# One attention and two-layer feed-forward kernel: state loads on other queues, ScalarE's opening held in order, two weight pieces converted earlier

## The chip, the cores and the metric

The kernel runs on one core of one Trainium2 chip. The metric is device time in microseconds (us) of one execution; three runs of the kernel before gave 1241.46, 1243.35 and 1245.03 us, so the median is 1243.35 us. The core has a matrix engine (TensorE, PE in the profile, with its weight loads as PEld), a vector engine (VectorE, DVE), a scalar engine (ScalarE, ACT), GpSimd (POOL) and SyncE (SP). SP, ACT and POOL can issue transfers (DMAs) between memory and the on-chip buffers; the same 16 DMA engines carry them all.

## The reference

```python
def _attn_ref(x, state):                       # x (8,8,512,64), state (8,8,32,64), float32
    scores = scale * x @ state^T;  a = softmax(scores);   xread = a @ state
    scores2 = scale * state @ x^T; a2 = softmax(scores2); sread = a2 @ x
    return concat([xread, sread], axis=2)      # 544 rows for each of 8 batches
# reshaped to (4352, 512), then
h = relu(x @ w_in);  y = (h * h) @ w_out       # 512 -> 2048 -> 512
c = (y @ w1) * (y @ w2);  out = (c @ w3) @ w_out2
```

The weights come as 64-bit floats. The kernel reads them as pairs of 32-bit words and converts them to float32 itself.

## The kernel before

**Tiling.** Token chunk `c` is one batch of 512 tokens (a ninth, of 256 columns, holds the states' rows). The hidden width 2048 is cut into 16 pieces of 128, `f`. `h_tile(c, f)` (matmuls on line 463) makes one piece of `x @ w_in`: since the attention output is `a @ state`, the kernel folds `state @ w_in` into one product `sw` (`make_sw`, line 433) and multiplies that by the transposed attention `aT`. `act_h` then applies relu (line 449) and square (line 451) on ScalarE and splits the result into a high and a low part, `ghl` (`split`, lines 84 on ScalarE and 85 on VectorE). `y_tile(c, f)` (line 501) multiplies `ghl` by a piece of `w_out`, held as `wo{f}`: three matmuls (high x high, low x high, high x low) for each of four outputs y0 to y3, 12 in all.

**Conversion.** A weight piece arrives as `raw` (`load64`, lines 119 and 121). `low_words` (line 131, ScalarE) scales the low words; four VectorE operations (`convert64`, lines 144, 145, 146, 149) put the float32 together. For a `w_out` piece the result is `cw` (two buffers), which `split` then turns into `wo{f}`. The first 512 columns of `w_in` are `win0`, loaded and converted in two halves of 256 columns and in two row groups: `make_win0(half, kk)`.

**The opening.** Lines 536 to 573: loads of x for batch 0, of the first half of `win0`, of the states (`load_st(0)`, eight loads, line 523), of the second half of `win0`, of `w_out` piece 0, of x for batch 1 and of the other states (`load_st(1)`), all issued by SP in that order. Then the steps of batch 0's attention: transposes of x (`xp`, copied to `xT` on line 294), states transposed (`stT`, line 533), scores `S`, the first softmax `e` (exp on line 342), its transpose split into `aT` (`at[0]`, `at[1]`).

**What sets the order.** Each engine works through its own list in order; the lists are made at build time from the order in which the code is written and from `tc.issue_after(x)`, under which an operation is placed no earlier than behind `x`. `order` (line 666) lists the pairs `(c, f)`; `side[i]` and `late[i]` hold jobs written beside pair `i`, among them `conv`, which takes the next piece of the list `convs`.

```python
side[0] = [lambda: make_win0(1, 0), lambda: make_win0(1, 1), s2[0]]
side[1] = [*xp1, lambda: make_sw(0, 0, slice(256, 512)), lambda: make_wout(0), a2t[0], s2[1], sc1]
side[2] = [conv, s1a1[0], a2t[1], s1b1[0], at1[0]]
```

So `win0`'s second half is converted first, its `sw` is made, and `w_out` pieces 0 and 1 are converted after that.

Of the kernel before, what the change touches and what calls it, by code (L numbers as in the profile page):

```python
# [12 lines left out]
ACTF = mybir.ActivationFunctionType  # L13
# [7 lines left out]
def kernel(  # L21
# [55 lines left out]
    def bank_y(d, name):  # L77
        return psum.tile([P, 512], F32, tag=f"y{d}", bufs=1, name=name)

    def split(hi, lo, src, hi_on_vector=False):  # L80
        if hi_on_vector:
            nc.vector.tensor_copy(hi, src)
        else:
            nc.scalar.copy(hi, src)  # L84
        return nc.vector.tensor_tensor(out=lo, in0=src, in1=f32(hi), op=ALU.subtract)  # L85

    PASSES = ((HI, HI), (LO, HI), (HI, LO))
# [34 lines left out]
        raws[key] = t  # L122

    lows = {}

    def low_words(key, t, scalar=True):
        r, lw = t[:, :, 0], t[:, :, 0].bitcast(U32)
        if key[0] == "win0":
            r = att.tile([P, 512], I32, tag="cw", bufs=2, name="cl")
        if scalar:  # L130
            nc.scalar.activation(r, lw, ACTF.Copy, scale=2.0**-29)
        else:
            nc.vector.tensor_single_scalar(r, lw, 2.0**-29, op=ALU.mult)
        lows[key] = r
# [29 lines left out]
    def make_win0(half, kk):  # L164
        if win_t[0] is None:
            win_t[0] = wpool.tile([P, ND, 512], F32, tag="wi0", bufs=2, name="win0")
        convert64(("win0", half, kk), win_t[0][:, 2 * kk:2 * kk + 2, half * 256:(half + 1) * 256])
# [111 lines left out]
    def att_steps(b):  # L279
# [5 lines left out]
        def xpose(k):  # L285
            ps = bank_m("ps_x") if b else bank_y(k, "ps_x")
            for j in range(J):
                h0 = 2 * (k % 2)
                nc.tensor.transpose(
                    ps[:, j * P:(j + 1) * P],  # L290
                    X[b, k // 2][:, j, h0:h0 + 2, :].rearrange("p h d -> p (h d)"), ident,
                )
            t = att.tile([P, 512], F32, tag="xT", bufs=4, name="xT")
            nc.scalar.copy(t, ps)
            xT[b, k] = t

        def scores():
            pss = [bank_m("ps_s") for _ in range(G)]
            for k in range(HG):
                for r in range(G):  # L300
                    rows = slice(r * D, (r + 1) * D)
                    nc.tensor.matmul(  # L302
                        pss[r][k * NS:(k + 1) * NS, :], stT[rows, b, k, :], xT[b, k][rows, :],
                        start=True, stop=True, tile_position=(r * D, k * NS),
                    )
            for r in range(G):
                s = att.tile([P, 512], F32, tag="S", bufs=2, name="S")
                nc.scalar.copy(s, pss[r])
                v["S", r] = s

        def soft2(r):
            nm = att.tile([P, 1], F32, tag="nm", bufs=2, name="nm")
# [26 lines left out]

        def soft1b(r):  # L340
            e = v["e1", r]
            nc.scalar.activation(e, e, ACTF.Exp, scale=scale)
            sm = att.tile([P, J * HG, 1], F32, tag="sm1", bufs=2, name="sm1")
            nc.vector.tensor_reduce(out=sm, in_=e, axis=AX.X, op=ALU.add)
            nc.vector.tensor_scalar_add(sm, sm, 1e-9)
            nc.vector.reciprocal(sm, sm)
            nc.vector.tensor_tensor(out=e, in0=e, in1=sm.to_broadcast([P, J * HG, NS]), op=ALU.mult)

        def a_T(r):
            e = v["e1", r].rearrange("p k n -> p (k n)")  # L350
# [166 lines left out]
    def load_st(half):  # L517

        t = raw_tile(True, f"st{half}").bitcast(F32).rearrange("p a b -> p (a b)")[:, :B * D]
        t = t.rearrange("p (b r d) -> p b r d", r=2, d=D)  # L520
        for k in range(HG):
            for r in range(G):
                nc.sync.dma_start(
                    t[k * NS:(k + 1) * NS, :, r, :],
                    state[half * (B // 2):(half + 1) * (B // 2), 2 * k + r].rearrange("b n d -> n b d"),
                )
        st.append(t.rearrange("p b r d -> p b (r d)"))
# [18 lines left out]
    load_wout(0, True)  # L546
    for g in range(G):
        load_x(1, g, True)
    load_st(1)
    for r in range(G):  # L550
        aT_t[2, r] = wpool.tile([P, 2, 512], F32R, tag="wo", bufs=NF, name=f"aT2{r}")
    xp, sc, s2, s1a, s1b, at, a2t, sr, srt = att_steps(0)
    xp1, sc1, s21, s1a1, s1b1, at1, a2t1, sr1, srt1 = att_steps(1)
    for step in xp:
        step()
    make_st(0)
    sc()
    make_win0(0, 0)
    make_win0(0, 1)
    s1a[0]()  # L560
    s1a[1]()
    s1b[0]()
    at[0]()
    s1b[1]()
    make_sw(0, 0, slice(0, 256), bank_y)
    idle = bank_h("idle")
    with tc.issue_after(last_sw[0].ins):
        for _ in range(16):
            nc.tensor.matmul(idle[:, :P], ident, ident, start=True, stop=True)
    first = at[1]()  # L570
    with tc.issue_after(first.ins):
        for g in range(G):
            make_x(1, g, nc.scalar, True)

# [30 lines left out]

    side = {i: [] for i in range(NF * B)}
    late = {}
    side[0] = [lambda: make_win0(1, 0), lambda: make_win0(1, 1), s2[0]]
    side[1] = [*xp1, lambda: make_sw(0, 0, slice(256, 512)), lambda: make_wout(0), a2t[0], s2[1], sc1]
    side[2] = [conv, s1a1[0], a2t[1], s1b1[0], at1[0]]  # L610
    side[3] = [conv, s21[0], sr, s1a1[1], srt, a2t1[0], conv, s1b1[1], sw(1, 0), at1[1]]
    side[4] = [conv, s21[1], lambda: make_st(1)]
    side[5] = [conv, a2t1[1]]
# [23 lines left out]
            side[i + 2].append(lambda b=b, g=g: load_xn(b, g))  # L637
    for _ in range(3):
        load_next()


    pend = []
# [26 lines left out]
    for i, (c, f) in enumerate(order):  # L669
        h_tile(c, f)  # L670

        gate = done[i - 3] if i >= 8 else first if i == 0 else None
        with tc.issue_after(gate.ins) if gate else nullcontext():
            for job in side.get(i, ()):
                job()
        if c == B - 1 and f == 11:
# [338 lines left out]
```

## Time and profile before

| | |
|---|---|
| median of three runs | 1243.35 us (1241.46 to 1245.03) |
| the profiled execution | 1244.7 us, of which the span of its trace is 1242.7 us |
| TensorE busy | 1226.2 us (99% of the span), weight loads 977.0 us (79%) |
| VectorE busy | 780.8 us (63%) |
| ScalarE busy | 623.9 us (50%) |
| GpSimd busy | 102.9 us (8%) |
| mean granted TensorE clock | 0.995 of full speed |
| chain that ended last | TensorE 94% of the span, DMA 2%, VectorE 2%, ScalarE 1% |

A matmul's busy time is modelled as lasting until its end, so a TensorE that reads as busy may be waiting between matmuls; how many matmuls end in a stretch, and the weight loads' busy time, say more. Times in the trace are us from the start of the span. An arrow `<-` behind an idle time names what ended it.

### The profile page before, as it was taken

The numbers are of one execution on the slowest core, as the hardware profiler recorded it, in microseconds if no ns is written. First come the engines' busy times: TensorE is split into PE (matmuls) and PEld (weight loads), VectorE is DVE, ScalarE is ACT, GpSimd is POOL, SyncE is SP. The second block draws the span as 40 slices with busy tenths as digits, with TensorE's granted clock in tenths as the row PEclk, the third lists the DMA queues.
The fourth block names the chain that finished last, engine by engine and source line by source line (L and its number), as shares of the span: only waits on it lengthen the run. The fifth ranks groups of instructions, "written<-read, shape, count | busy, mean of one in ns | idle before, by whom it ended". The sixth has DMA issues, their size and how long they took to land.

```text
span 1242.7 us, 17483 instructions
## 1 busy us (share of the span) xinstructions
PE 1226.2 (99%) x6608; PEld 977.0 (79%) x6608; DVE 780.8 (63%) x1406; ACT 623.9 (50%) x1129; POOL 102.9 (8%) x158
## 2 busy tenths in 40 slices
PE   6999999999999999999999999999999999999998
PEld 4677777777777777777799888888888888887886
DVE  6987877677686766642346835555755548475753
ACT  6777556565464645545556534444443534333330
POOL 0000001232421101100000000102400010000000
PEclk9999999999999999999999999999999999999999
DMA  7354655744645363201423520404430522323213
GB/s 237 103 187 152 170 149 174 164 130 103 153 123 145 119 141 129 71 18 34 102 69 119 203 85 1 152 17 152 120 136 17 204 68 65 139 88 117 84 52 118
DMA packets 124179, 143.22 MB, mean 115 GB/s; under 512 B 72640, under 2 KB 76224, under 8 KB 123584
## 3 DMA queue, kind: packets, MB, share of 16 engines
q1 hardware_dynamic: 114368, 110.65, 29.6%
q0 software_dynamic: 9728, 31.47, 8.1%
q8 instruction: 51, 0.84, 0.3%
q14 instruction: 32, 0.26, 0.1%
HBM read 96.47 MB, written 45.61 MB: 114 GB/s over the span
## 4 chain that ended last, share of the span: by engine, by line
PE 94%; DMA 2%; DVE 2%; ACT 1%; SPq 1%; issue 0%; DVEq 0%
PE y L501 30%; PE po L910 13%; PE qa L829 10%; PE qd L829 7%; PE ps_w L714 4%; PE qc L829 3%; PE qe L829 3%; PE ps_sw L433 3%; PE ab L884 2%; DMA x<-in_x_dram 1%; PE ps_s L302 1%; DMA out_dram<-o 1%; DVE yq L85 1%; PE ps_r L379 1%; PE ps_a L371 1%; DMA st<-in_state_dram 0%
## 5 line engine op out<-in xcount | busy, mean ns | idle before, releaser
L501 PE MATMUL y<-ghl,wo 128*128 128x512 f32 (+1 forms) x1728 | 402.5, 381 | 0.3 <-ACT wo L84 0.2
L501 PEld LDWEIGHTS y<-ghl,wo 128*128 128x128 f32 x1728 | 309.3, 188 | 87.1 <-ACT r L449 15.1
L85 DVE TENSOR_TENSOR ghl<-r,ghl 128x512 fp32r<-128x512 f32 (+1 forms) x144 | 94.7, 658 | 161.3 <-ACT ghl L84 158.2
L829 PE MATMUL qa<-yq,wq 128*128 128x512 f32 x576 | 146.4, 390 | 0.8 <-ACT s L837 0.8
L837 ACT COPY s<-qa 128x512 f32<-128x512 f32 x96 | 56.2, 589 | 143.8 <-PE qa L829 131.2
L829 PEld LDWEIGHTS qa<-yq,wq 128*128 128x128 f32 x576 | 107.5, 188 | 24.8 <-ACT s L837 1.7
L829 PE MATMUL qd<-yq,wq 128*128 128x512 f32 x384 | 98.2, 390 | 0.0
L910 PE MATMUL po<-w34b,c 128*128 128x512 f32 x408 | 95.8, 391 | 0.3 <-DVE o L919 0.3
L910 PE MATMUL po<-w,c 128*128 128x512 f32 x408 | 95.4, 391 | 0.0
L910 PEld LDWEIGHTS po<-w34b,c 128*128 128x128 f32 x408 | 75.7, 188 | 18.0 <-DVE c L85 1.0
L451 ACT ACTIVATE r<-r 128x512 f32<-128x512 f32 (+1 forms) x144 | 87.8, 610 | 3.3
L910 PEld LDWEIGHTS po<-w,c 128*128 128x128 f32 x408 | 75.5, 188 | 17.7 <-ACT o L916 1.1
L84 ACT CAST ghl<-r 128x512 fp32r<-128x512 f32 (+1 forms) x144 | 86.2, 598 | 3.7
L829 PEld LDWEIGHTS qd<-yq,wq 128*128 128x128 f32 x384 | 71.8, 188 | 15.5 <-ACT s L837 0.8
L841 DVE TENSOR_TENSOR s<-qa,s 128x512 f32<-128x512 f32 x32 | 22.1, 692 | 74.5 <-ACT s L837 74.5
L787 POOL TENSOR_TENSOR yraw<-yraw,yp 128x512 f32<-128x512 f32 x24 | 32.2, 1345 | 436.2 <-DMA yraw<-yscr 305.8
L84 ACT CAST c<-s 128x512 fp32r<-128x512 f32 x64 | 39.7, 622 | 36.4 <-DVE s L858 35.4
L84 ACT CAST yq<-yraw 128x512 fp32r<-128x512 f32 x70 | 42.6, 623 | 21.4 <-DVE yraw L804 15.5
L919 DVE TENSOR_TENSOR o<-po,opart 128x512 f32<-128x512 f32 x34 | 23.3, 689 | 46.4 <-PE po L910 34.8
L85 DVE TENSOR_TENSOR c<-s,c 128x512 fp32r<-128x512 f32 x64 | 48.3, 773 | 2.1
L829 PE MATMUL qc<-yq,wq 128*128 128x512 f32 x192 | 49.5, 390 | 0.0
L829 PE MATMUL qe<-yq,wq 128*128 128x512 f32 x192 | 49.2, 389 | 0.0
(561 smaller groups left out, 1809.8 us busy)
## 6 DMA issues: line engine op xcount, KB each, us to landing
yraw<-yscr SPq DMA_DIRECT2D x56, 256.0 KB, 5.1
yscr<-yo SPq DMA_DIRECT2D x52, 256.0 KB, 2.7
oscr<-o SPq DMA_DIRECT2D x34, 256.0 KB, 2.0
opart<-oscr SPq DMA_DIRECT2D x34, 256.0 KB, 2.9
raw<-in_moe_w_out_dram SPq DMA_DIRECT2D x16, 512.0 KB, 4.6
raw<-in_moe_w_dram POOLq DMA_DIRECT2D x64, 128.0 KB, 3.4
raw<-in_moe_w_dram POOLq DMA_DIRECT2D x16, 512.0 KB, 4.3
out_dram<-o SPq DMA_DIRECT2D x32, 256.0 KB, 2.9
```

What stands on the lines that cost most here:

```text
L84: nc.scalar.copy(hi, src)
L85: return nc.vector.tensor_tensor(out=lo, in0=src, in1=f32(hi), op=ALU.subtract)
L433: mm = nc.tensor.matmul(pss[r][k * NS:(k + 1) * NS, cols], stT[rows, b, k, :], win_t[fg][rows, k, cols], start=True, stop=True, tile_posit ...
L451: nc.scalar.activation(r[:, :n], r[:, :n], ACTF.Square)
L501: nc.tensor.matmul(y_ps[c, d][:, :n], wo_t[f][:, wi, d * P:(d + 1) * P], t[:, gi, :n], start=(f == f0 and k == 0), stop=(f == f1 - 1 and k ...
L714: nc.tensor.matmul(ps, t[:, wi, (j % 4) * P:(j % 4 + 1) * P], wo2_t[j][:, vi, :], start=(j == 0 and k == 0), stop=(j == N1 - 1 and k == 2),)
L787: nc.gpsimd.tensor_tensor(out=t[:, n], in0=t[:, n], in1=p, op=ALU.add)
L829: nc.tensor.matmul(ps, W[w, kt][:, wi, m * P:(m + 1) * P], Y[v, kt][:, vi, :], start=(first and kt == 0 and k == 0), stop=(last and kt == ...
L837: nc.scalar.copy(t, ps)
L884: nc.tensor.matmul(pss[i][:, :NT9], w[:, wi, m * P:(m + 1) * P], Y[B, d][:, vi, :NT9], start=(d == 0 and k == 0), stop=(d == ND - 1 and k ...
L910: nc.tensor.matmul(ps, v[:, vi, t * P:(t + 1) * P], w[:, wi, :], start=(m == 0 and k == 0), stop=(m == QM - 1 and k == 2),)
L919: nc.vector.tensor_tensor(out=o, in0=ps, in1=o_in.pop((c, t)), op=ALU.add)
```

## The change

1. `load_st` no longer uses SP. Of the first eight state loads four go to ScalarE's queue and four to GpSimd's; the other eight all go to GpSimd's. `load_st(1)` is written later, after three `load_next()`.
2. Low-word operations of the early pieces are placed with `issue_after` behind named ScalarE operations: the two of `win0`'s first half behind the last `xT` copy and the last `S` copy, those of `win0`'s second half and of `w_out` piece 0 behind the second exp, those of `w_out` pieces 1 to 3 behind the last high part of `aT`. The copies of x for batch 1 follow the second exp instead of `at[1]`.
3. `w_out` pieces 0 and 1 (`make_wout(0)`, `conv`, `close_splits`) move to `side[0]`; `win0`'s second half moves to `side[1]`. All side jobs of the first eight pairs come behind `at[1]`.

```diff
 def split(hi, lo, src, hi_on_vector=False):
...
-            nc.scalar.copy(hi, src)
+            his.append(nc.scalar.copy(hi, src))
...
 def low_words(key, t, scalar=True):
         r, lw = t[:, :, 0], t[:, :, 0].bitcast(U32)
+        gate = gates.pop(key, None)
...
         if scalar:
-            nc.scalar.activation(r, lw, ACTF.Copy, scale=2.0**-29)
+            with tc.issue_after(gate.ins) if gate else nullcontext():
+                nc.scalar.activation(r, lw, ACTF.Copy, scale=2.0**-29)
...
 def load_st(half):
...
         for k in range(HG):
+            queue = nc.scalar if half == 0 and k < 2 else nc.gpsimd
             for r in range(G):
-                nc.sync.dma_start(
+                queue.dma_start(
...
     for g in range(G):
         load_x(1, g, True)
-    load_st(1)
...
     for step in xp:
-        step()
+        gates["win0", 0, 0] = step()
     make_st(0)
-    sc()
+    gates["win0", 0, 1] = sc()
     make_win0(0, 0)
     make_win0(0, 1)
     s1a[0]()
     s1a[1]()
     s1b[0]()
     at[0]()
-    s1b[1]()
+    last = s1b[1]()
+    for key in (("win0", 1, 0), ("win0", 1, 1), ("wo", 0)):
+        gates[key] = last
     make_sw(0, 0, slice(0, 256), bank_y)
...
     first = at[1]()
-    with tc.issue_after(first.ins):
+    for f in range(1, 4):
+        gates["wo", f] = his[-1]
+    with tc.issue_after(last.ins):
         for g in range(G):
             make_x(1, g, nc.scalar, True)
...
-    side[0] = [lambda: make_win0(1, 0), lambda: make_win0(1, 1), s2[0]]
-    side[1] = [*xp1, lambda: make_sw(0, 0, slice(256, 512)), lambda: make_wout(0), a2t[0], s2[1], sc1]
-    side[2] = [conv, s1a1[0], a2t[1], s1b1[0], at1[0]]
+    side[0] = [lambda: make_wout(0), conv, close_splits, s2[0]]
+    side[1] = [*xp1, lambda: make_win0(1, 0), lambda: make_win0(1, 1)]
+    side[1] += [lambda: make_sw(0, 0, slice(256, 512)), a2t[0], s2[1], sc1]
+    side[2] = [s1a1[0], a2t[1], s1b1[0], at1[0]]
...
     for _ in range(3):
         load_next()
+    load_st(1)
...
-        gate = done[i - 3] if i >= 8 else first if i == 0 else None
-        with tc.issue_after(gate.ins) if gate else nullcontext():
+        gate = done[i - 3] if i >= 8 else first
+        with tc.issue_after(gate.ins):
             for job in side.get(i, ()):
```

The steps `xpose`, `scores` and `soft1b` now return their last ScalarE operation, so that it can be named as a gate.

ScalarE's list between the copies of the scores `S` and the second `aT` before the change (`cl` and `raw` on line 131 are low words of `win0` and of `w_out`; `X` are the copies of x for batch 1):

```order
L308 COPY S<-ps_s 128x512 x2
L131 ACTIVATE cl<-raw 128x512 x2
L84 CAST sw_264<-ps_sw 128x256
L84 CAST sw_267<-ps_sw 128x256
L131 ACTIVATE raw<-raw 128x512
L342 ACTIVATE e_216<-e_216 128x512
L342 ACTIVATE e_225<-e_225 128x512
L240 COPY X_0_295<-x_0_140 128x1024
L240 COPY X_1_297<-x_1_142 128x1024
```

The same place after it, to the last operation ahead of the first relu (line 457 there); two `sw` casts are left out:

```order
L314 COPY S<-ps_s 128x512 x2
L136 ACTIVATE cl<-raw 128x512
...
L349 ACTIVATE e_207<-e_207 128x512
L349 ACTIVATE e_216<-e_216 128x512
L245 COPY X_0_286<-x_0_140 128x1024
L245 COPY X_1_288<-x_1_142 128x1024
L136 ACTIVATE raw<-raw 128x512
L299 COPY xT<-ps_x 128x512
L86 CAST aT_236<-ps_a 128x512
L299 COPY xT<-ps_x 128x512
L86 CAST aT_283<-ps_a 128x512
L136 ACTIVATE raw<-raw 128x512 x3
```

One low word of `win0` has moved from in front of the `S` copies to behind them; the low words of the second half of `win0` and of piece 0 no longer stand in front of the exps; piece 0's stands behind the copies of x, and those of pieces 1 to 3 stand between the second `aT` and the first relu.

TensorE's list behind the first two `h_tile` products before the change, where `ps_sw` is the product for `win0`'s second half:

```order
L289 MATMUL ps_x<-ident,X_1_297 128x128 x7
L433 MATMUL ps_sw<-win_203,stT 32x256 x8
L463 MATMUL ph_2__433<-aT_245,sw_264 128x512
L463 MATMUL ph_3__507<-aT_245,sw_264 128x512
L463 MATMUL ph_2__433<-aT_245,sw_264 128x512 x2
L463 MATMUL ph_2__433<-aT_292,sw_267 128x512 x3
```

And after it:

```order
L294 MATMUL ps_x<-ident,X_1_288 128x128 x6
L509 MATMUL y_494<-ghl,wo_324 128x512
L509 MATMUL y_495<-ghl,wo_324 128x512
L509 MATMUL y_496<-ghl,wo_324 128x512
L509 MATMUL y_497<-ghl,wo_324 128x512
L509 MATMUL y_494<-ghl,wo_324 128x512 x2
L509 MATMUL y_495<-ghl,wo_324 128x512 x2
L509 MATMUL y_496<-ghl,wo_324 128x512 x2
L509 MATMUL y_497<-ghl,wo_324 128x512 x2
L509 MATMUL y_494<-ghl,wo_336 128x512 x3
L509 MATMUL y_495<-ghl,wo_336 128x512 x3
```

All 24 `y` matmuls of pieces 0 and 1 now stand between the transposes and the `ps_sw` product, which the third and fourth `h_tile` need.

## Rows read from the trace of the kernel before

**Rows 1.** Busy time by stretch (windows); the first line names the columns.

```profile
core 0: us, PE busy (x) PEld busy (x) DVE busy (x) ACT busy (x) POOL busy (x), PEclk, DMA share, GB/s
25.00:30.00 5.00, 3.09 (x22) 2.03 (x20) 5.00 (x12) 4.14 (x8) 0.00 (x0) 0.94 0.88 351
29.00:30.00 1.00, 0.86 (x8) 0.33 (x8) 1.00 (x3) 1.00 (x3) 0.00 (x0) 0.68 0.40 160
30.00:37.00 7.00, 7.00 (x31) 4.71 (x26) 5.42 (x17) 4.49 (x11) 0.00 (x0) 0.56 0.00 1
40.00:47.00 7.00, 5.99 (x30) 4.41 (x29) 6.97 (x16) 5.01 (x10) 0.00 (x0) 1.00 0.19 66
47.00:60.00 13.00, 12.84 (x133) 8.59 (x132) 12.22 (x29) 10.74 (x20) 0.00 (x0) 1.00 0.60 190
100.00:150.00 50.00, 49.99 (x316) 37.87 (x315) 40.61 (x78) 29.89 (x53) 0.00 (x0) 1.00 0.61 176
```

**Rows 2.** Chain that ended last, opening: start, length, engine, tile, line.

```profile
2.79 5.71 DMA st<-in_state_dram
...
12.33 9.02 DMA x<-in_x_dram
21.38 1.05 ACT X L240
...
29.14 2.08 PE ps_sw L433 x16
...
36.92 1.82 PE ps_s L302 x16
```

**Rows 3.** Timeline of SP's queue: start, length, what was issued, how often.

```profile
2.79 5.70 SPq L523 DMA_DIRECT2D st<-in_state_dram  x8
...
13.54 8.14 SPq L523 DMA_DIRECT2D st<-in_state_dram  x8
21.73 2.11 SPq L121 DMA_DIRECT2D raw<-in_moe_w_out_dram  x3
```

**Rows 4.** Windows of one us; the last two columns are DMA share and GB/s.

```profile
8.00:9.00 1.00, 1.00 (x7) 0.95 (x5) 0.69 (x2) 0.75 (x2) 0.00 (x0) 1.00 0.17 35
9.00:10.00 1.00, 0.20 (x2) 0.00 (x0) 0.86 (x2) 1.00 (x3) 0.00 (x0) 1.00 0.44 121
21.00:22.00 1.00, 0.94 (x8) 0.58 (x6) 0.97 (x3) 0.62 (x1) 0.00 (x0) 1.00 0.10 23
```

**Rows 5.** Groups of POOL's instructions: count, busy us, mean ns, idle before.

```profile
L210 POOL DMA_DIRECT2D raw<-in_moe_w_dram x64 | 34.4, 544 | 42.8 <-DVE cw L149 25.0 <-DVE xT L264 17.3 <-issue 0.2
```

**Rows 6.** Timeline of ScalarE, 16 to 26 us.

```profile
16.36 0.68 ACT L131 ACTIVATE cl<-raw 128x512 int32<-128x512 uint32 x1 [0.80 <-DVE mx L336]
16.94 0.63 ACT L84 CAST sw<-ps_sw 128x256 fp32r<-128x256 f32 x2
17.61 0.68 ACT L131 ACTIVATE raw<-raw 128x512 int32<-128x512 uint32 x1
18.18 1.13 ACT L342 ACTIVATE e<-e 128x512 f32<-128x512 f32 x2
...
21.38 1.05 ACT L240 COPY X<-x 128x1024 f32<-128x1024 f32 x1 [1.12 <-DMA x<-in_x_dram]
...
23.76 0.61 ACT L84 CAST aT<-ps_a 128x512 fp32r<-128x512 f32 x1
...
25.82 0.60 ACT L449 ACTIVATE r<-ph__305 128x512 f32<-128x512 f32 x1 [1.45 <-PE ph__305 L463]
```

**Rows 7.** Timeline of VectorE, first and last of eight conversions of `win0`.

```profile
25.01 0.75 DVE L144 TENSOR_SCALAR win<-raw 128x512 f32<-128x512 f32 x2
...
28.76 0.68 DVE L149 CUSTOM_DVE_ANT_0 win<-win,cl 128x1024 uint16<-128x1024 uint16 x1
```

**Rows 8.** Timeline of TensorE's matmuls.

```profile
26.31 0.93 PE L289 MATMUL ps_x<-ident,X 128*128 128x128 f32 x7
...
34.31 2.18 PE L463 MATMUL ph__507<-aT,sw 128*128 128x512 f32 x5
...
40.87 5.05 PE L501 MATMUL y<-ghl,wo 128*128 128x512 f32 x19
...
72.72 2.99 PE L501 MATMUL y<-ghl,wo 128*128 128x512 f32 x12
```

More of the change, by code (lines that the diff above doesn't have):

```diff
@@ L78, in bank_y @@
         return psum.tile([P, 512], F32, tag=f"y{d}", bufs=1, name=name)
+    his = []
     def split(hi, lo, src, hi_on_vector=False):
@@ L124 @@
     lows = {}
+    gates = {}
     def low_words(key, t, scalar=True):
         r, lw = t[:, :, 0], t[:, :, 0].bitcast(U32)
+        gate = gates.pop(key, None)
         if key[0] == "win0":
@@ L293, in xpose @@
             t = att.tile([P, 512], F32, tag="xT", bufs=4, name="xT")
-            nc.scalar.copy(t, ps)
+            last = nc.scalar.copy(t, ps)
             xT[b, k] = t
+            return last
         def scores():
@@ L307, in scores @@
                 s = att.tile([P, 512], F32, tag="S", bufs=2, name="S")
-                nc.scalar.copy(s, pss[r])
+                last = nc.scalar.copy(s, pss[r])
                 v["S", r] = s
+            return last
         def soft2(r):
@@ L341, in soft1b @@
             e = v["e1", r]
-            nc.scalar.activation(e, e, ACTF.Exp, scale=scale)
+            last = nc.scalar.activation(e, e, ACTF.Exp, scale=scale)
             sm = att.tile([P, J * HG, 1], F32, tag="sm1", bufs=2, name="sm1")
@@ L347, in soft1b @@
             nc.vector.tensor_tensor(out=e, in0=e, in1=sm.to_broadcast([P, J * HG, NS]), op=ALU.mult)
+            return last
         def a_T(r):
```

## The prediction

> **What bounds the kernel now.** I read the busy times by stretch first. From 100 us on TensorE is the bound: it is busy 49.99 of 50 us, with weight loads 76% of the time and VectorE at 81% [rows 1]. Nothing in the change alters that work, so whatever it brings is won or lost in the first 75 us or so, where the same view shows TensorE fed badly: its weight loads fill 63% of the stretch 40 to 47 us and 66% of 47 to 60 us, and VectorE is busy 6.97 of 7 us and 12.22 of 13 us [rows 1]. So from 40 us VectorE sets the pace, and it can only be helped by starting its queue earlier or by taking out idle time before 40 us: from 30 to 37 us it is idle 7.00 - 5.42 = 1.6 us [rows 1].
>
> The second thing to see is TensorE's clock. Its transposes end at 27.24 us, the next work, `ps_sw`, starts at 29.14 [rows 2, 8]; after this pause of 1.9 us the granted clock is 0.68 in the stretch 29 to 30 us and 0.56 in 30 to 37 us [rows 1], that is the lower of its two levels (0.5, 1.2 GHz) for about 0.6 + 6.2 = 6.8 us. Matmuls of 512 columns take 2.18 / 5 = 0.436 us there and 2.99 / 12 = 0.25 us at the full clock [rows 8].
>
> The third view is the chain, which in the opening runs through transfers: the states (5.71 us) and then the second half of x for batch 1 (9.02 us, to 21.35) [rows 2]. SP's queue says why: two groups of eight state loads hold it for 5.70 and 8.14 us, and pieces 1 to 3 of `w_out` are not issued before 21.73 [rows 3]. Meanwhile the DMA engines have little to do: 0.17 and 0.44 busy in 8 to 10 us, 0.10 in 21 to 22 us [rows 4].
>
> **The states on other queues.** Sixteen issues leave SP. Four go in front of ScalarE's `xT` copies. No row shows an issue by ScalarE; SP's eight take 5.70 / 8 = 0.71 us each with their waits [rows 3], and bare ones nothing at the least, so 0 to 2.8 us between the warm-up operation and the first copy; I take 2 us. They stand where ScalarE waited for `win0` anyway, so this is hidden; without that cover it would move the whole opening by up to 2 us. Twelve go to GpSimd at 0.54 us each [rows 5], 6.5 us on an engine with no other work in these stretches [rows 1]. The gain is in the stream: the idle 0.83 + 0.56 = 1.4 us of 8 to 10 us [rows 4] fill, less what the second group of state packets, now ahead of x, takes. I take 1.0 us earlier for x of batch 1, at 20.3 us; bounds 0 and 1.4. Pieces 1 to 3 of `w_out` gain more, since the pause at 21 us goes too [rows 4]: I estimate the third at 24 to 25 us.
>
> By the Trainium skill, "DMA: Bandwidth & Descriptors", section "Issuing engines are not separate DMA queues", transfers started from several engines still share the same DMA engines, so that spreading them saves only the time spent on issuing. Here that issuing is what rows 3 and 4 show as the cost, so the rule does not forbid a gain; where the engines are already full it makes the gain nothing, x lands at 21.35 as before, and the sum below would be 1.1 us worse.
>
> **ScalarE's opening.** Two low words leave from in front of the exps: one in front of the `sw` casts (16.94 - 16.36 = 0.58 us) and one behind them (18.18 - 17.61 = 0.57 us) [rows 6]. Up to 1.15 us is gained. The low word of `win0` that now stands behind the `S` copies delays the `sw` casts; I give 0.5 us back for it. So the exps end 0.65 us earlier and the second x copy waits for its data until 20.3 instead of 21.38 [rows 6], but piece 0's low word (0.6 us) now follows it. The second `aT`, at 23.76 before [rows 6], comes at 23.3: 1.1 - 0.6 = 0.5 us earlier. Bounds: 0.6 us later (x lands no earlier) to 0.8 us earlier (x no longer waited for, all 1.4 us won).
>
> Behind it stand three low words, 3 x 0.6 = 1.8 us, in front of the first relu. That relu waited 1.45 us for TensorE until 25.82 [rows 6]. The three run from 23.85 to 25.65, so they are covered as long as the third piece is there by 25 us. Queued behind them are both relus, the squares and `ghl`, and for these wait the `y` matmuls.
>
> **The two pieces first.** VectorE's eight conversions took 25.01 to 29.44 with one 0.6 us `ghl` operation between [rows 7], so 3.8 us; the same eight for pieces 0 and 1 start 0.5 us earlier and end at 28.3. ScalarE now does relu, relu, square, square, `ghl`, `wo`: six starts 0.55 us apart from 25.65 bring the first `wo` high part at about 28.9. TensorE's transposes end at 26.7, so it pauses 2.2 us, about as before (1.9). I therefore take the low clock as before, 6.8 us from 28.9: 6.8 / 0.436 = 16 of the 24 `y` matmuls run low, 8 at 0.25, to 37.8 us. Then `ps_sw`, 2.08 / 2 = 1.0 us at full clock [rows 2], 12 `ph` matmuls 3.0, `ps_s` 1.8 [rows 2], three groups of transposes 1.8: 45.4 us. The kernel before has finished the same set at 40.87 + 5.05 = 45.9 [rows 8]. Gain 0.5 us.
>
> If the clock stayed full, the 24 `y` would end at 34.9, VectorE's work for `win0`'s second half (from about 31.5, 4.4 us) at 35.9, and the set at 36.0 + 7.6 = 43.6: gain 2.3 us. If the low stretch lasted until the set is done, 24 x 0.436 = 10.5, 2.1, 5.2, and 3.6 or more would bring it to 50: a loss of 4. I take 0.5, the value nearest to the rows.
>
> From 47 us VectorE has 13.00 - 12.22 = 0.8 us idle [rows 1]; with pieces 2 and 3 converted in one go I take this as won, bounds 0 and 0.8. The lists hold the same operations otherwise, so nothing else is added or removed.
>
> **Sum.** 0.5 (it holds the opening's 0.5, since the set starts from it) + 0.8 = 1.3 us. Against the profiled execution, 1244.7 us (span 1242.7 and 2.0 around it), that is 1243.4; the median of the runs lies 1.35 us below the profiled one, so I forecast 1243.35 - 1.3 = 1242.0 us. A run of this kernel can tell a difference of about 0.3%, 3.7 us, from no change; the forecast lies inside.
>
> **Rivals.**
> - *The clock stays up.* The `y` matmuls are 24 dense ones and might not see the low level for long. For it: the pause is no longer than before and work comes denser behind it. Against: the pause is there. Gain 2.3 + 0.8, and 0.8 at most from the opening in place of 0.5: with x's whole 1.4 us some 4.0 in all: 1239.3 us.
> - *Given back.* x lands no earlier, or VectorE, full from 40 us [rows 1], waits for `sw` behind the `y` matmuls what it won before: 1243.4 us.
> - *ScalarE held at the third low word.* If the third piece of `w_out` lands late, both relus wait behind its low word although their matmuls are done. Before, the last of the three was issued at about 23.4 [rows 3], and the stream ran full to 29 us (0.88 of 25 to 30 us, 0.40 in the last us) [rows 1]. Landing at 28 us, the low word ends at 28.65, 3.0 us late; TensorE pauses 5 us, and all 24 `y` and `ps_sw` run low: 8 x 0.186 + 1.0 = 2.5 us more. -1.3 + 3.0 + 2.5 = +4.2: 1247.6 us. It costs from a landing after 25 us, and decides the sign from about 26. Against it: SP issues these loads behind 14 others and no state load, with the pauses gone.
>
> **How the numbers follow.** Forecast (within 1.3 us of no change or a little better) 0.42, given back 0.19, clock stays up 0.25, ScalarE held 0.14. The forecast alone has 1240.5 to 1244.0. The range 1237.6 to 1247.0 leaves out about one in ten on each side. Faster by over 0.3% is most of the first rival and a tail of the forecast: 0.26; slower by over 0.3% most of the held case: 0.13; the rest, 0.61, no change.
>
> **What would show it.** Right: no state load on SP and its `w_out` loads issued before 15 us; DMA share high throughout 8 to 10 us; the second `aT` cast at 23.0 to 23.6; the first `y` at 28.5 to 29.3; a low clock of about 7 us behind a pause of 2 us; the last `y` of piece 1 at 37 to 38.5 and the second `e` transposes of batch 0 done by 45.5; after 100 us the same rows. Wrong: ScalarE idle in front of a low word of pieces 1 to 3; a clock at full level from 29 to 37; x of batch 1 landing after 21.3; VectorE idle for more than 2 us between 36 and 40.

## The result, and the profile after the change

The changed kernel takes 1250.0 us (median of 6 runs, 1249.44 to 1251.23), the kernel before on the same chip 1243.67 us: 6.3 us slower, ratio 1.0053 (1.0042 to 1.0065). I had forecast 1242.0 us; the result lies outside my range.

The busy times by stretch, columns as in [rows 1], the first two stretches new:

```profile
5.00:10.00 5.00, 3.65 (x16) 3.14 (x16) 1.80 (x3) 2.19 (x4) 3.07 (x5) 1.00 1.10 298
25.00:30.00 5.00, 3.82 (x20) 2.89 (x18) 4.59 (x10) 5.00 (x11) 0.00 (x0) 1.00 0.00 0
30.00:37.00 7.00, 5.78 (x24) 4.41 (x24) 6.86 (x16) 6.01 (x12) 0.00 (x0) 1.00 0.27 75
40.00:47.00 7.00, 6.54 (x40) 3.97 (x40) 6.97 (x16) 6.24 (x12) 0.00 (x0) 1.00 0.44 139
47.00:60.00 13.00, 11.05 (x119) 6.86 (x117) 12.72 (x33) 12.11 (x23) 0.00 (x0) 1.00 0.60 180
60.00:65.00 5.00, 1.88 (x11) 1.36 (x10) 2.60 (x6) 1.63 (x3) 0.00 (x0) 0.89 0.78 287
100.00:150.00 50.00, 50.00 (x316) 37.87 (x315) 39.34 (x80) 32.02 (x57) 0.00 (x0) 1.00 0.59 179
```

After 100 us nothing has changed. Between 25 and 37 us the clock is full, where before fell to 0.56 [rows 1]; no gain is left of that in the end. Most of the loss shows from 47 us on: TensorE is busy 11.05 of 13 us (12.84 before) and then 1.88 of 5 us, all engines with it. Before was busy throughout that last stretch:

```profile
60.00:65.00 5.00, 5.00 (x32) 3.81 (x29) 5.00 (x13) 5.00 (x12) 0.00 (x0) 1.00 0.53 162
```

The chain that ended last, in the changed kernel (start, length, what), tells where to look:

```profile
1.53 5.57 DMA st<-in_state_dram
7.38 4.78 DMA st<-in_state_dram
12.48 0.89 PE ps_st L541 x4
...
35.31 1.19 DVE win L151 x2
...
37.26 1.21 PE ps_sw L441 x16
...
51.67 5.08 DMA x<-in_x_dram
56.77 1.05 ACT X L245
57.84 5.33 DMA raw<-in_moe_w_out_dram
63.26 0.68 ACT raw L136
63.94 0.48 ACT aT L86
```

In place of one round of states and x [rows 2] there are two rounds of states, then the halves, and from 51.67 us transfers that are not on the chain of before: the second half of x for batch 2, its copy, which frees a buffer, the load of `w_out` piece 4 into that buffer, its low word on ScalarE, and behind it the second `aT` of batch 1.

**How the loss adds up.** I take three marks: the second `aT` of batch 0, the first transposes of batch 1's scores (`ps_n`), and the second `aT` of batch 1. Before has them at 23.76 [rows 6] and here (timeline):

```profile
10.30 0.63 PE L532 MATMUL ps_st<-ident,st 128*128 128x128 f32 x4 [1.10 <-DMA st<-in_state_dram]
39.79 0.66 PE L333 MATMUL ps_n<-ident,S 128*128 128x128 f32 x4
57.74 0.59 ACT L84 CAST aT<-ps_a 128x512 fp32r<-128x512 f32 x1 [0.17 <-PE ps_a L357]
58.70 0.71 ACT L131 ACTIVATE raw<-raw 128x512 int32<-128x512 uint32 x1
```

The timeline of the changed kernel (start, length, engine, line, what; in brackets the idle time in front and what ended it):

```profile
12.48 0.88 PE L541 MATMUL ps_st<-ident,st 128*128 128x128 f32 x4 [2.95 <-DMA st<-in_state_dram]
25.46 0.61 ACT L86 CAST aT<-ps_a 128x512 fp32r<-128x512 f32 x1
25.94 1.82 ACT L136 ACTIVATE raw<-raw 128x512 int32<-128x512 uint32 x3
27.64 0.61 ACT L457 ACTIVATE r<-ph__305 128x512 f32<-128x512 f32 x1
28.00 0.82 PE L294 MATMUL ps_x<-ident,X 128*128 128x128 f32 x6
30.92 5.78 PE L509 MATMUL y<-ghl,wo 128*128 128x512 f32 x24 [2.09 <-ACT wo L86]
37.26 1.15 PE L441 MATMUL ps_sw<-win,stT 64*32 64x256 f32 x16 [0.56 <-DVE win L154]
39.98 1.89 PE L308 MATMUL ps_s<-xT,stT 64*32 64x512 f32 x16
43.08 0.60 PE L340 MATMUL ps_n<-ident,S 128*128 128x128 f32 x4
43.88 1.41 PE L471 MATMUL ph__510<-aT,sw 128*128 128x512 f32 x5
57.84 0.33 SPq L123 DMA_DIRECT2D raw<-in_moe_w_out_dram  x1
63.26 0.68 ACT L136 ACTIVATE raw<-raw 128x512 int32<-128x512 uint32 x1 [3.27 <-DMA raw<-in_moe_w_out_dram]
63.83 0.57 ACT L86 CAST aT<-ps_a 128x512 fp32r<-128x512 f32 x1
64.46 1.22 PE L471 MATMUL ph__659<-aT,sw 128*128 128x512 f32 x2 [2.92 <-ACT aT L86]
```

- Opening: 25.46 - 23.76 = 1.70 us late; the states land 2.2 us later (`ps_st` at 12.48, not 10.30).
- From there to `ps_n`: 17.62 us, before 16.03: 1.59 us.
- From `ps_n` to the second `aT` of batch 1: 20.75, before 17.95: 2.80 us. ScalarE stands 3.27 us in front of piece 4's low word; in before that low word came behind the `aT` (58.70 against 57.74).

Together 6.09 us, and the medians differ by 6.3. The marks of before come from one execution, at 1244.7 us 1.0 us above its median here, so the close match is partly chance. I call the three terms the states, the order and piece 4; the experiments test them, and the second does not show as a cost at the end.

### The profile page after: what moved, and what is told of

The parts are those of the page before. It is cut to its first block, busy times and chain, and to the rows that moved or that the text cites. A ratio compares the mean times of both kernels' runs of the same rounds, so it can differ in the third digit from the quotient of the medians.

```text
span 1248.1 us, 17500 instructions
## 1 busy us (share of the span) xinstructions
PE 1224.7 (98%) x6608; PEld 975.6 (78%) x6608; DVE 778.0 (62%) x1406; ACT 623.3 (50%) x1129; POOL 111.4 (9%) x170
## 4 chain that ended last, share of the span: by engine, by line
PE 95%; DMA 2%; ACT 2%; DVE 1%; issue 0%; SPq 0%; POOL 0%; POOLq 0%; ACTq 0%
PE y L509 30%; PE po L924 15%; PE qa L843 10%; PE qd L843 7%; PE qc L843 4%; PE ps_w L728 3%; PE qe L843 3%; PE ps_sw L441 3%; PE ab L898 2%; DMA st<-in_state_dram 1%; PE ps_s L308 1%; PE ps_r L387 1%; PE ps_a L379 0%; DMA raw<-in_moe_w_out_dram 0%; DMA x<-in_x_dram 0%; DMA yraw<-yscr 0%
## 5 line engine op out<-in xcount | busy, mean ns | idle before, releaser
L933 DVE TENSOR_TENSOR o<-po,opart 128x512 f32<-128x512 f32 x34 | 23.3, 689 | 46.4 <-PE po L924 39.6
L87 DVE TENSOR_TENSOR yq<-yraw,yq 128x512 fp32r<-128x512 f32 x70 | 46.7, 684 | 2.8 <-ACT yq L86 2.6
```

Of the source, the lines that this page charges most:

```text
L933: nc.vector.tensor_tensor(out=o, in0=ps, in1=o_in.pop((c, t)), op=ALU.add)
```

## Experiments

All runs in one table: the time is the median less that of before on the same chip, with the interval of the ratio; the marks are from one profiled execution each. `aT` to `aT` is the time from the second `aT` of batch 0 to that of batch 1. The last column is the start of `ph__1162`, a product of `h_tile` that every version reaches near 100 us; the differences between the versions there are still the same, within 0.15 us, at another such product (`ph__3301`) near 313 us.

| run | time, us | ratio, 95% | `ps_st` | 2nd `aT`, batch 0 | `ps_n` | 2nd `aT`, batch 1 | `aT` to `aT` | at 100 us |
|---|---|---|---|---|---|---|---|---|
| before | 0 | | 10.30 | 23.76 | 39.79 | 57.74 | 33.98 | 100.18 |
| after | +6.3 | 1.0042-1.0065 | 12.48 | 25.46 | 43.08 | 63.83 | 38.37 | 106.03 |
| e1 | +3.2 | 1.0020-1.0036 | 12.54 | 25.36 | 42.95 | 61.00 | 35.64 | 102.11 |
| e2 | +6.4 | 1.0037-1.0063 | 12.18 | 25.85 | 43.94 | 64.19 | 38.34 | 105.29 |
| e3 | +6.7 | 1.0038-1.0066 | 9.96 | 22.70 | 45.20 | 64.08 | 41.38 | 106.83 |
| e4 | +2.9 | 1.0013-1.0032 | 12.60 | 26.28 | 41.26 | 59.91 | 33.63 | 102.49 |
| e5 | +4.4 | 1.0019-1.0044 | 9.84 | 23.03 | 40.44 | 60.86 | 37.83 | 103.21 |
| e6 | +2.0 | 1.0005-1.0022 | 9.71 | 22.75 | 40.09 | 58.26 | 35.51 | 99.37 |
| e7 | +1.3 | 1.0002-1.0019 | 9.85 | 22.98 | 38.23 | 56.88 | 33.90 | 99.34 |
| e8 | +2.1 | 1.0004-1.0022 | 9.95 | 23.41 | 41.51 | 59.62 | 36.21 | 100.59 |
| e9 | +2.4 | 1.0011-1.0033 | 10.00 | 23.68 | 41.81 | 59.77 | 36.09 | 102.28 |
| e10 | +3.8 | 1.0026-1.0051 | 12.31 | 25.98 | 44.08 | 61.35 | 35.37 | 103.42 |
| e11 | 0.0 | 0.9994-1.0014 | 9.81 | 22.69 | 37.26 | 56.27 | 33.58 | 98.58 |
| e12 | +3.9 | 1.0019-1.0044 | 12.62 | 25.85 | 43.07 | 60.91 | 35.06 | 102.76 |
| e13 | +1.8 | 1.0007-1.0024 | 10.00 | 24.07 | 41.01 | 59.28 | 35.21 | 101.01 |
| e14 | +2.5 | 1.0018-1.0036 | 9.91 | 23.06 | 39.01 | 56.88 | 33.82 | 100.78 |
| e15 | +1.7 | 1.0008-1.0026 | | | | | | |
| e16 | +4.9 | 1.0030-1.0059 | 9.91 | 23.91 | 43.32 | 63.38 | 39.47 | 104.56 |

**e1, piece 4 held behind the second `aT` of batch 1.**

```diff
-    side[3] = [conv, s21[0], sr, s1a1[1], srt, a2t1[0], conv, s1b1[1], sw(1, 0), at1[1]]
+    side[3] = [conv, s21[0], sr, s1a1[1], srt, a2t1[0], conv, s1b1[1], sw(1, 0), held]
+    def held():
+        gates["cv4"] = at1[1]()
+        gates["wo", 4] = his[-1]
 def make_wout(f):
-        convert64(("wo", f), w)
+        with tc.issue_after(gates.pop("cv4").ins) if f == 4 else nullcontext():
+            convert64(("wo", f), w)
```

> The changed kernel with one edit: the low word and the first VectorE step of w_out piece 4 are placed behind the second aT of batch 1, on ScalarE and on VectorE. Theory A (the fifth piece: ScalarE waits 3.27 us and VectorE 1.93 us for it with that aT queued behind, TensorE idles 2.92 us and then runs low): aT at 60.5 to 61.5 us instead of 63.83, no wait of TensorE over 1.5 us between 60 and 65, median 3 to 5 us below the changed kernel, 1245 to 1247. Theory B (the states land 2 us later and the whole opening is late): nothing before 60 us differs, so the median stays within 1 us of 1250. Theory C (the order of the two halves itself costs): also within 1 us of 1250.

Half the loss is gone. ScalarE's timeline, where the low word now follows the `aT`, which waits for TensorE alone:

```profile
61.00 0.59 ACT L86 CAST aT<-ps_a 128x512 fp32r<-128x512 f32 x1 [1.16 <-PE ps_a L366]
62.16 0.69 ACT L136 ACTIVATE raw<-raw 128x512 int32<-128x512 uint32 x1
```

The opening is as late as in after (25.36), and 18.05 us pass from `ps_n` to the `aT`, as in the kernel before (17.95). So the wait is a cause, worth 3.1 us here, and not the only one.

**e2, the first eight state loads back on SP.**

```diff
-            queue = nc.scalar if half == 0 and k < 2 else nc.gpsimd
+            queue = nc.sync if half == 0 else nc.gpsimd
```

> The changed kernel with one edit: the first eight state loads go back to SP, in their old place; the other eight stay on GpSimd. Theory B: the transposes of the states start at about 10.3 instead of 12.48 us, the second aT of batch 0 at 23.3 to 23.8 instead of 25.46, and the median falls by 1.5 to 2.5 us to 1247.5 to 1248.5. Theory A: the opening moves, but the wait for w_out piece 4 remains, since its load hangs on a buffer; the median falls by less than 1 us, and the wait of ScalarE for that piece grows by what the opening won.

It did not do what it was for: the states came as late as ever. The timeline shows what still goes out ahead of them: GpSimd has nothing else to issue, and the second eight loads, first used near 60 us, start at 1.53.

```profile
1.53 4.78 POOL L532 DMA_DIRECT2D st<-in_state_dram  x8 [0.22 <-issue]
2.79 6.86 SPq L532 DMA_DIRECT2D st<-in_state_dram  x8
12.18 1.09 PE L541 MATMUL ps_st<-ident,st 128*128 128x128 f32 x4 [2.73 <-DMA raw<-in_moe_w_in_dram]
```

**e3, the order of the halves alone, on the kernel before** (part 3 of the change, with its gate).

```diff
-    side[0] = [lambda: make_win0(1, 0), lambda: make_win0(1, 1), s2[0]]
+    side[0] = [lambda: make_wout(0), conv, close_splits, s2[0]]
+    side[1] = [*xp1, lambda: make_win0(1, 0), lambda: make_win0(1, 1)]
...
-        gate = done[i - 3] if i >= 8 else first if i == 0 else None
+        gate = done[i - 3] if i >= 8 else first
```

> The kernel before with part 3 alone: w_out pieces 0 and 1 ahead of the second half of win0, all states on SP, no gates on low words. In its ScalarE list the low word of piece 4 stands ahead of the second aT of batch 1, as in the changed kernel. Theory A: slower than the kernel before by 3 to 5 us, 1246.5 to 1249, with that wait in the trace. Theory B: no slower than 1 us (the states are where they were). Theory C: slower by 5 us or more, with or without the wait.

The whole loss with early states. But it is not the wait that I had named: ScalarE stands only 0.96 us in front of piece 4's low word. Pieces 1 to 3 are still issued at 20.7 us behind the states, so this holds another wait (the `y` matmuls wait 2.29 us for `wo` at 33.66). The terms are not additive over the parts of the change: each part was covering or uncovering another's wait.

**e4, the change without the order.**

```diff
-    side[0] = [lambda: make_wout(0), conv, close_splits, s2[0]]
+    side[0] = [lambda: make_win0(1, 0), lambda: make_win0(1, 1), s2[0]]
...
```

> The changed kernel without part 3: states on the other queues and the gates, but win0's second half first as before; here the low word of piece 4 stands behind the second aT. Theory B: slower than the kernel before by 1.5 to 2.5 us, 1245 to 1246.5, with the states' transposes at 12 to 12.5 us. Theory A: within 1 us of the kernel before, since nothing waits for piece 4. Theory C: within 1 us of the kernel before.

It loses 2.9 us, with the opening 2.5 us late and `aT` to `aT` as in before (33.63). That points to the lateness as a cost of its own; e7 takes it away from this run.

**e5 to e7: states early, and then the other terms taken away one by one.** All sixteen state loads go on SP again, the second eight behind pieces 1 to 3. e6 adds the edit of e1; e7 has the old order of the halves (the edit of e4).

```diff
-            queue = nc.scalar if half == 0 and k < 2 else nc.gpsimd
+            queue = nc.sync
```

> The kernel after with all sixteen state loads on SP's queue: the first eight at the place that they have before the change, the other eight behind the third of pieces 1 to 3, so that these pieces are still issued early. The order of the halves stays, and so does piece 4's low word ahead of the second aT of batch 1. If the late states are one cost of their own (theory B, about 3 us from the run without the order), the first ps_st transposes are back at about 10.2 us, the second aT of batch 0 comes at 22.8 to 23.8, and the time is about 1247 us, with the stall at 58 to 64 us still there. If piece 4's wait alone sets the end (theory A: its transfer is tied to the load of x for batch 2, and a late opening is swallowed by it), the opening is back but the second aT of batch 1 still comes near 63.5 us and the time stays at 1249 to 1250 us. If the order itself is the cost (theory C), also 1249 to 1250, but with less than 1 us of waiting for piece 4.

> As the run before, and piece 4's low word and conversion are held behind the second aT of batch 1. The new order of the halves and the new order of ScalarE's opening stay. Theories A and B together: no wait for piece 4, states at about 10.2 us, second aT of batch 1 at 58 to 59 us; 1243 to 1245 us, the time of the kernel before or a little over. Theory C (the order itself costs): 1246.5 us or more with both waits gone.

> The kernel after without its third part (the halves converted in the order of before), and with the state loads on SP as in the two runs before this one. Theory B: the 2.9 us that the change lost without its third part were the states' lateness, so this comes back to 1243 to 1245 us, second aT of batch 1 near 57.7 us. If ScalarE's held order is what costs there, it stays at 1246.5 to 1248 us with the states early.

Timeline of e5: against e2 only the second eight loads have moved, from GpSimd at 1.5 us to SP at 15 us, and the first are there 2.3 us sooner. Of these, 1.5 us lie in SP's own issuing of the first eight: 5.35 us here, 6.86 us in e2.

```profile
2.79 5.35 SPq L532 DMA_DIRECT2D st<-in_state_dram  x8
9.84 0.78 PE L541 MATMUL ps_st<-ident,st 128*128 128x128 f32 x4 [0.57 <-DMA st<-in_state_dram]
14.96 0.43 SPq L532 DMA_DIRECT2D st<-in_state_dram  x1
```

Without the states the loss is 4.4, without piece 4 3.2, without both 2.0 us: each is worth 1.2 to 1.9 and 2.4 to 3.1 us. In the old order the states are worth 1.6 us (e4 against e7). At 100 us the same pairs agree better: 2.7 to 3.2 us for the states, 3.8 to 3.9 for piece 4.

The order is another matter. `aT` to `aT` is 35.5 us in e6 and 33.9 in e7, but that lateness is made up again. `ph__1162` in before, after, e6 and e7:

```profile
100.18 1.64 PE L463 MATMUL ph__1162<-aT,sw 128*128 128x512 f32 x6
106.03 1.64 PE L471 MATMUL ph__1162<-aT,sw 128*128 128x512 f32 x6
99.37 1.64 PE L472 MATMUL ph__1162<-aT,sw 128*128 128x512 f32 x6
99.34 1.64 PE L471 MATMUL ph__1162<-aT,sw 128*128 128x512 f32 x6
```

e6 and e7 differ in the order (piece 4's low word is behind the second `aT` in both) and are level here; so nearly are e1 and e4 (102.11, 102.49). In time the new order is 0.7 and 0.3 us behind, too little to tell from nothing.

The clock hides in this comparison: e6 ran at full clock from 25 to 40 us, e7 at 0.77. The executions of before that were timed beside the experiments show what that can be worth: 23 with a mean granted clock of 1.000 took 1242.5 us on average, 35 with 0.997 or less 1245.0, and on each of the five chips the gap is 2.4 to 3.1 us. (Where in an execution the clock was low is known for the profiled one alone.) So the new order may cost some 2 us and get them back from a clock that stays up; no run parts the two.

**e8, x of batch 2 later** (e6 with the second half's load moved from `side[3]` to `side[5]`, so that piece 4 is asked for first).

```diff
-        side[2 + g].append(lambda g=g: (load_x(2, g), make_x(2, g, nc.scalar)))
+        side[2 + 3 * g].insert(1 if g else len(side[2]), lambda g=g: (load_x(2, g), make_x(2, g, nc.scalar)))
```

> As the run with both undone, and the load of the second half of x for batch 2 moved two steps later, so that w_out piece 4 is asked for ahead of it. Theory A says that piece 4's transfer, issued at 57.8 us because its buffer stood behind that load and its copies, is then issued some 4 to 6 us earlier; with the wait already taken off the second aT of batch 1 by the other edit this should be worth little more: 1241.5 to 1244 us, at best 1 to 2 us under the run with both undone. If VectorE's conversions behind it were waiting for piece 4 too, the gain is up to 3 us. If x of batch 2 is wanted sooner than that (its turning waits), the time is 1 to 3 us longer than the run with both undone.

Piece 4 was issued at 51.87, 3.1 us sooner than in e6, and the time is that of e6. Once the `aT` does not stand behind it, its arrival is worth nothing.

**e9 and e10, three pieces of the next weight held too** (e6 and e1 with `win` pieces 1 to 3 of column group 1 behind the second `aT` of batch 1).

```diff
 def make_win(fg, k):
-        convert64(("win", fg, k), win_t[fg][:, k, :])
+        key = ("win", fg, k)
+        with tc.issue_after(held_conv.pop(key).ins) if key in held_conv else nullcontext():
+            convert64(key, win_t[fg][:, k, :])
...
```

> The kernel after with the states back on SP (the second eight behind pieces 1 to 3), w_out piece 4 held behind the second aT of batch 1, as in the run with both undone, and now also three of the four first-weight pieces of the next column group (the second to the fourth) held behind that aT. Theory C, made definite by the run with both undone: there the set with the first y's ends 3 us ahead of before (first y of the next segment at 42.8 against 45.9), but VectorE is busy for 19.57 of the 20 us from 40 to 60 and carries 110 instructions ahead of that aT where before carries 98, the excess being two and a half weight pieces of 2.0 to 2.4 us; so the 3 us are spent in VectorE's list. If so, the second aT of batch 1 comes at 53.5 to 55.5 us (58.3 with both undone, 57.7 before), and the time is 1241 to 1244 us. If TensorE's own order and not VectorE's list holds that aT, it stays at 57.5 us or later and the time at 1245 to 1246 us. If the held pieces are what TensorE wants next, it waits for them between 56 and 66 us, and the time is 1245 us or more with the aT early.

> As the run before, with the states left where the change puts them (ScalarE's and GpSimd's queues, late). It shows what the late states cost once neither piece 4 nor VectorE's list sets the end: theory B says 1.7 to 2.4 us over the run before, so about 1244 to 1246 us, second aT of batch 1 about 2.5 us later than there; if the lateness is swallowed by another wait, the two runs are within 1 us.

VectorE's list behind 40 us as the price of the order fell. VectorE is now idle in the stretch in question (it was busy 9.81 of these 10 us in e6), and the `aT` comes no sooner (59.77):

```profile
50.00:60.00 10.00, 7.35 (x82) 4.21 (x71) 6.38 (x17) 8.29 (x17) 0.00 (x0) 0.89 0.81 249
```

The late states cost 3.8 - 2.4 = 1.4 us between the two (1.1 us at 100 us), less than I expected.

**e11, the kernel before with only its second eight state loads later** (`load_st(1)` behind the three `load_next()`).

> The kernel before with one edit: its second eight state loads, still on SP, stand behind pieces 1 to 3 of w_out instead of ahead of them. It parts the run without the order and with early states (1244.8 us, 1.2 us over before) into this move and ScalarE's held order. If the move alone is worth nothing: 1243 to 1244.3 us, and the 1.2 us are ScalarE's held order or nothing that can be told from before. If the earlier pieces fill the queues against the first weight's halves: 1244.5 to 1246 us.

No change (1.0004). Yet its second `aT` of batch 1 is 1.5 us earlier than before's, and at 100 us it is 1.6 us ahead. Part of this is the choice of executions: the profiled one of before is 1.0 us above its median, that of e11 0.8 us below its own (1243.46, 1244.23). So a microsecond on the marks against before says nothing of the medians.

e7 and e11 differ in the held order of ScalarE's opening and in the side jobs' place behind `at[1]`. e7 is 1.3 us slower in time and 0.8 us behind at 100 us; their intervals overlap, and no run takes these edits alone. By the medians, the way from after over e5, e6 and e7 to e11 is 1.9 us for the states, 2.4 for piece 4, 0.7 for the order with its clock and 1.3 for this rest. The states show in four pairs and piece 4 in two; the last two terms are not clear of noise.

**e12 and e13, batch 1's scores ahead of the `y` matmuls** (the changed kernel, and e6). **e14**, the same on e11 with the old order.

```diff
-    side[0] = [lambda: make_wout(0), conv, close_splits, s2[0]]
+    side[0] = [*xp1, sc1, lambda: make_wout(0), conv, close_splits, s2[0]]
...
```

> The kernel after with one edit: in the lists of side work the transposes of x and the scores (ps_s) of batch 1 stand ahead of the conversion of pieces 0 and 1, so that the 16 matmuls of ps_s go ahead of the 24 y's on TensorE. States late, and piece 4 as in after. Theory D, read from eleven traces: the new order puts y's ahead of ps_s, the head of batch 1's chain; ps_s starts at 39.98 us in after (36.85 before), the first aT of batch 1 comes 10.6 to 11.1 us behind it in all of them, the second 20.5 to 21.3 us behind it (23.5 to 23.9 where piece 4's low word waits), and the medians follow that second aT. By D ps_s runs at 28 to 31 us, in the pause of 2.1 us ahead of the first y; what follows it on TensorE (ps_n) still stands behind the y's, so that of the 10 us some 3 come through: first aT of batch 1 at 46.5 to 49 us, second at 57 to 60, time 1244.5 to 1247.5 us. If the place of ps_s is only a sign of other work (VectorE's list, or the late states alone), the first aT stays within 1 us of 51.1 and the time at 1249 to 1250.5 us.

> The run with both undone (states early on SP, piece 4 held behind the second aT of batch 1), and the scores of batch 1 ahead of y's as in the run before this one. Theory D: ps_s at 25 to 28 us, first aT of batch 1 at 44 to 46.5, second at 54.5 to 57 (58.3 with both undone); 1241 to 1244 us, at best 2 us under the kernel before. If VectorE is the bound from 40 to 60 us (19.57 of 20 us busy with both undone), the second aT stays at 57.5 to 58.5 and the time at 1244.5 to 1246 us.

> The kernel before with its second state loads behind pieces 1 to 3, as in the run that had this edit alone (1244.2 us), and batch 1's scores moved ahead of the first weight's second half on TensorE; the halves keep the order of before. If the early start of batch 1's chain is worth something whatever the order of the halves, its second aT comes ahead of 56.3 us and the time is 1240 to 1243 us. If from there on something else sets the end (TensorE was never idle from 57 us on in the run with that edit alone, and it gained nothing from a second aT 1.5 us earlier), the aT is earlier and the time stays at 1243 to 1245 us.

My theory that `ps_s` heads the chain fell as well. TensorE's timeline in e12: `ps_s` runs 11 to 13 us earlier, and `ps_n` behind it starts at 43.07, in the changed kernel at 43.08.

```profile
27.30 1.04 PE L308 MATMUL ps_s<-xT,stT 64*32 64x512 f32 x2
28.69 1.08 PE L308 MATMUL ps_s<-xT,stT 64*32 64x512 f32 x14
43.07 0.49 PE L340 MATMUL ps_n<-ident,S 128*128 128x128 f32 x3
```

The first `aT` of batch 1 did not come earlier either (52.27 against 51.11), but here ScalarE stood directly in front of it for a low word of the first weight:

```profile
51.66 0.72 ACT L136 ACTIVATE raw<-raw 128x512 int32<-128x512 uint32 x1 [2.22 <-DMA raw<-in_moe_w_in_dram]
```

e13 has no such wait, and its first `aT` is no earlier than that of e6 (48.86, 48.17); its time is that of e6 too. e12 gains 2.4 us; in its list piece 4's low word is behind the second `aT` once more, as in e1. The time fell in the expected window for another reason than the expected one. e14 misses both of its windows: 2.5 us slower than before, though its second `aT` is 0.9 us early. TensorE pauses for 3.33 us ahead of `ps_sw`, in before for 1.91:

```profile
32.33 1.08 PE L433 MATMUL ps_sw<-win,stT 64*32 64x256 f32 x8 [3.33 <-ACT S L308]
```

The clock is 0.66 from 30 to 40 us, and at 100 us e14 is 2.2 us behind e11.

**e15 and e16: only piece 0 ahead of the halves, and the halves first with both pieces right behind them** (both on e6).

```diff
-    side[0] = [lambda: make_wout(0), conv, close_splits, s2[0]]
+    side[0] = [lambda: make_wout(0), close_splits, s2[0]]
...
```

```diff
-    side[0] = [lambda: make_wout(0), conv, close_splits, s2[0]]
+    side[0] = [lambda: make_win0(1, 0), lambda: make_win0(1, 1), lambda: make_wout(0), conv, close_splits, s2[0]]
...
```

> The run with both undone, but with only the first w_out piece converted ahead of the first weight's second half; the second piece goes back behind it, where before has it. Over the traces so far the time from the second aT of batch 0 to the second aT of batch 1 is 33.6 to 34.0 us with the old order of the halves (whatever the states, the clock and the place of the scores) and 35.1 to 36.2 us with the new one when piece 4 doesn't wait (35.5 with both undone). If this price of the order is VectorE's: the piece of about 2.3 us each that stands ahead of the halves and so ahead of the second half of sw (split on VectorE at 35.90 us with both undone, 31.01 in before), one piece instead of two halves it: 34.4 to 35.0 us, the sw split near 33.5 us, and 1243.5 to 1245 us. If the price is that y's go ahead of the other work on TensorE, it stays at 35.1 to 36.2 and 1245 to 1246.5 us.

> The run with both undone, with the first weight's second half converted first again and the two w_out pieces right behind it, ahead of batch 1's scores, so that 12 y's still go early on TensorE. If VectorE's order of conversions is the price: 33.6 to 34.3 us from aT to aT, sw's second half split at 30 to 31.5 us, and 1242.5 to 1244.5 us. If early y's on TensorE are the price: 35 us or more and 1245 to 1246.5 us.

e15 cannot be told from e6 in time; its profiled execution, 1250.8 us, is the longest of its twelve, so its marks are left out. e16 is the surprise: the halves first, and 4.9 us lost. TensorE's timeline and the stretch:

```profile
29.77 0.66 PE L295 MATMUL ps_x<-ident,X 128*128 128x128 f32 x4 [2.80 <-ACT xT L300]
33.41 5.08 PE L510 MATMUL y<-ghl,wo 128*128 128x512 f32 x12
```

```profile
30.00:38.00 8.00, 7.68 (x33) 4.67 (x32) 8.00 (x21) 5.15 (x11) 0.00 (x0) 0.57 0.22 67
```

A pause of 2.8 us, then the low clock, and 12 `y` matmuls at 0.42 us each in front of the `ph` products that the chain needs; from 60 to 65 us the clock is low again (0.50). All six executions of e16 have a mean clock of 0.994 to 0.997, those of e6 0.997 to 1.000, so e16 does not part the early `y` from the clock. The halves come first in it and `aT` to `aT` is still 39.5 us, which speaks against VectorE's order of conversions as the only price.

So `aT` to `aT` is 35.1 to 36.2 us in the new order (e1, e6, e8 to e10, e12 and e13) and 33.6 to 34.0 in the old; but that the early `y` on TensorE do this is argued, not shown. `ps_n` starts without idle time in front of it in after, e6, e12, e13 and e16: its place in TensorE's list holds it, behind `ps_sw` and `ph` products. But `ps_sw` itself waits 0.56 us in after and 0.33 us in e6, behind the last `y`, for VectorE's `win`. There the `y` work and VectorE's conversions end almost together, and either would have held the chain.

## Why the prediction was wrong

Two steps failed. The sum had no term for the landing of the states themselves (1.2 to 1.9 us by the medians), and behind 47 us it held that "nothing else is added or removed" (piece 4: 2.4 to 3.1 us).

- **The states (step "this is hidden").** This failed first. I priced the issue time on ScalarE and the earlier x of batch 1, and no term for the states' own landing, though the chain showed the states at its head [rows 2]. x was indeed no longer waited for, as forecast; the second `aT` of batch 0 came at 25.46 where I had 23.3 with 24.4 as the late bound. Two things stand in the trace: ScalarE's fourth load goes out only at 6.91 us, and twelve loads start from GpSimd at 1.5 us, eight of them for data first used near 60 us. e2 takes the first away and the states are still late, so the second is enough; the first was not tested alone. The DMA engines that [rows 4] shows idle at 8 to 10 us were filled (1.10 in 5 to 10 us) with what was not needed yet. The rule that I quoted from the Trainium skill, "DMA: Bandwidth & Descriptors", section "Issuing engines are not separate DMA queues", that loads of several engines share the same DMA engines, agrees with e2 and e5. They differ in the place of the second eight loads alone, and the first use of the states is at 12.18 against 9.84 us. I had drawn from the rule that the gain could be nothing; it was a loss.
- **The three low words behind the second `aT`.** Right: three in 1.82 us from 25.94, without a wait, pieces landed in time (no transfers in 25 to 30 us).
- **The set of TensorE work.** The sum was right, 45.3 us (43.88 + 1.41) against my 45.4, by luck: the first `y` starts 2.0 us late (30.92, not 28.9), the 24 `y` take 3.1 us less than forecast (5.78, not 8.9) since the clock stayed full behind a pause of 2.1 us, and about 1 us more goes by behind them. The end of the set as the measure is not refuted: with the states and piece 4 undone, e6 is not behind before's profiled execution, with its low clock, at 100 us (99.37, 100.18), although its second `aT` of batch 1 is 0.5 us late.
- **Beyond 47 us.** Here I had only VectorE's 0.8 us. The largest term lies there: piece 4's low word changed places with the second `aT`. My third rival had the mechanism (ScalarE held by a low word whose piece lands late) at the wrong piece; I looked at pieces 1 to 3, and piece 4 is issued at the same time as before (57.84, 57.60), only its place in ScalarE's list is new. The order of ScalarE's list alone would have shown it.
- **The rival "the clock stays up".** Its condition came true and its 1239.3 us did not. The price of 2.3 us for the clock is close to the 2.5 us between before's executions at full and at low clock; what the rival left out are the states, piece 4 and what the new order may cost. Its sum was off as well: 2.3 + 0.8 + 0.3 is 3.4 and not 4.0 us, since the bound of 0.8 for the opening holds x's 1.4 us already.
- **Given back.** Not what happened: x landed early enough, and the loss lies in the states and piece 4, which this rival does not have.

No version beat before: the best, e11, equals it.

## What to carry to other kernels

Judge a reordering by marks well behind it, and not by one operation: e6 and e7 are 1.4 us apart at the second `aT` of batch 1 and level at 100 us. Compare executions of like clock before a mark of one is held against a mark of another. Where an in-order engine has an operation that waits for a transfer, look through the whole list for what it now stands in front of, far beyond the place of the edit. Loads that move to an idle queue start at once, so a load that is needed late belongs behind those needed first.

## What was not expected of the hardware

TensorE paused 1.9 us in before and the granted clock fell to 0.68 and 0.56 behind it [rows 1, 8]; it paused 2.1 us in after (28.82 to 30.92) and stayed at 1.00; in e16 it paused 2.8 us and fell to 0.57. The length of the pause alone does not tell. Executions of one and the same kernel fall on either side: those of before at a mean clock of 1.000 were 2.5 us faster on average than those at 0.997 or less.
